# Agent attention and a leaky MLP on one core: the conversions, subtractions and load order of the head, and where the second batch's keys begin

## The chip, the cores and the metric

The kernel runs on 1 core of one Trainium2 chip. The metric is device microseconds of an execution. The kernel before took 1010.07 us as the median of 3 runs (1010.05, 1010.07, 1012.32).

## The reference

```python
scale = 1.0 / np.sqrt(q.shape[-1])
def sm(a, b):
    s = scale * (a @ b.transpose(0, 2, 1))
    s = s - s.max(-1, keepdims=True)
    e = np.exp(s)
    return e / (e.sum(-1, keepdims=True) + 1e-09)
agent_v = sm(agents, k) @ v
x = (sm(q, agents) @ agent_v).reshape(B * S, D)
h = x @ w_in
out = np.maximum(0.01 * h, h) @ w_out
```

q, k and v are (2, 12480, 128) in float32, agents (2, 49, 128). w_in (128 x 2048) and w_out (2048 x 128) arrive as float64 bit patterns and are converted to float32 on the chip.

## The kernel before, in words

The second attention is folded into the MLP. For each batch the kernel needs `agent_v`, multiplies it into `w_in` (m_hi and m_lo, each value split into a rounded part and a rest) and then runs the MLP on 480 queries at a time. There are 26 such blocks per batch, 52 in all, and each is 8 steps of TensorE work. A step is `mm1` (two column tiles of h into a PSUM pair), `relu` (the rounded part on ScalarE, L708, and the rest on VectorE, L709) and, two steps later, `mm2` (L725, L735). A table called `side` hangs all other work on steps. Within a step, mm1 comes first, then the side work, then the mm2 of two steps before.

**The aux tile.** The PSUM pool `ps_x` has one buffer, two banks wide, named aux. The score products of the queries (`q_mm`, L595) take all of it at step 2 of every block. ScalarE then copies one half (`q_x`, L602) and VectorE adds the other (`q_add`, L608), and only then is the buffer free. The second batch's key scores (`k_score`, L359), the transposes of its maximum (`k_max1`, L391; `k_max2`, L403) and the products of its softmax with v (`k_av2`, L451, read by two VectorE additions, L459) use the same buffer.

**The second batch beside the first.** While batch 0's blocks run, one chunk of batch 1's keys is scored per block, at step 5. Then come its maximum and, spread evenly over the steps that remain, 26 halves (13 chunks) of subtraction, exponential and splitting, with `k_av2` 7 steps behind each second half. K1 = 2 of the 13 key chunks are scored already in the head, so 11 blocks carry keys and the 26 halves spread over U = 100 steps, four steps apart.

**The head.** Before the first block everything of batch 0 is made at once. 13 key tiles (480 KB each) are scored on TensorE (L359), VectorE keeps a running maximum (`k_run`, L370), and ScalarE copies the scores (L373). The maximum goes through `k_max0` to `k_max3`. Each chunk then has the maximum subtracted (`k_sub`, L325), its exponential taken (`k_exp`, L417), and is multiplied with its v tile (`k_av32`, L475; 13 tiles of 520 KB). Meanwhile eight tiles of the weights (512 KB each) are converted: `conv_bits` (L242, L243), `conv_exp` (L251, L252), `conv_mant`, `conv_low` (L256), `conv_sign` (L271), `conv_mul` (L278), and `wo_hi_of` for each w_out tile. The first queries go through their own chain (`chain`). At the end `f_copy`, `f_den`, `f_tr`, `f_rec` and `f_avT` finish agent_v, and `m_mm`, `m_hi_of` and `m_lo_of` make m from it. Key, v and weight tiles share nine buffers (`ld`), so a late load waits until an earlier tile has been read.

The order of the head is written by a small planner (`Plan`). Each step has an engine, a cost and the steps it follows; `emit` picks again and again the step that can begin first. The order of loads is given by hand in the string `ORDER`. In the kernel before, a step may have several engines with a cost each, and the planner takes the one that would end first. TensorE's gaps are filled with dummy products (`heat`, L841).

Of the kernel before, what the change touches and what calls it, by code (L numbers as in the profile page):

```python
# [18 lines left out]
class Plan:  # L19
# [6 lines left out]
    def add(self, name, eng, cost, fn, args, after):  # L26
        costs = eng if isinstance(eng, dict) else {eng: cost}
        self.steps[name] = costs, fn, args, after, isinstance(eng, dict)

    def emit(self, engines, idle):  # L30

        tail = {}

        users = {name: [] for name in self.steps}
        for name, step in self.steps.items():
            for a in step[3]:
                users[a].append(name)

        def rest(name):
            if name not in tail:  # L40
                tail[name] = min(self.steps[name][0].values()) + max(
                    (rest(u) + self.hop for u in users[name]), default=0
                )
            return tail[name]

        done = self.done
        while len(done) < len(self.steps):
            best = None
            for name, (costs, fn, args, after, pick) in self.steps.items():
# [3 lines left out]
                end, eng = min((max(ready, self.free[e]) + c, e) for e, c in costs.items())  # L53
                key = max(ready, self.free[eng]), name not in self.first, -rest(name)
                if best is None or key < best[0]:
                    best = key, name, eng, end
            (begin, *_), name, eng, end = best
            _, fn, args, _, pick = self.steps[name]
            if eng == idle[0] and begin > self.free[eng] + idle[2]:
                idle[1](round((begin - self.free[eng]) / idle[2]))  # L60
            fn(*args, *([engines[eng]] if pick else []))
            self.free[eng] = done[name] = end


@with_exitstack
def tile_agent_attention_then_leaky_mlp(
# [55 lines left out]

    ORDER = "kkkwkkkwkkwkkwkkwkwwqvvwvvvvqvvvvvvvq"
    LOWS = "pddddddd"
    K1 = 2
    HOP = 90
# [125 lines left out]
    def conv_low(n):  # L254
# [4 lines left out]
        )  # L259

    def conv_low1(n, eng):
        m_t[n] = rp.tile([P, MC], F32, tag="hi", name="wl")
        scale(eng, m_t[n], w_t[n][:, :, 0].bitcast(U32), 2.0**-52)

    def conv_low2(n):
        w = w_tile(n)
        nc.gpsimd.tensor_tensor(out=w, in0=w, in1=m_t.pop(n), op=ALU.add)

# [516 lines left out]
    for b in range(1, B):  # L785
        i0 = (b - 1) * BPB
        n0 = i0 + NCH - K1
        for c in range(K1, NCH):
            s = NP * (i0 + c - K1)
            for d in range(c, min(c + 3, NCH)) if c == K1 else (c + 2,) if c + 2 < NCH else ():  # L790
# [30 lines left out]
    with tc.manual_schedule():  # L821
# [28 lines left out]
        for o, a, n in SLOTS:  # L850
# [5 lines left out]

        add = plan.add
        fetch = {
            "k": (lambda c: load_k(0, c), 1120), "v": (lambda c: load_v(0, c), 1220),
# [22 lines left out]
        for n in range(2 * NM):  # L882
            r = [("mul", n - RP)] if n >= RP else []
            add(("bits", n), "dve", 900, conv_bits, (n,), [("w", n)] + r)
            add(("mant", n), {"act": 620, "pool": 730}, None, conv_mant, (n,), [("bits", n)])
            add(("exp", n), "act", 1300, conv_exp, (n,), [("bits", n)])
            if LOWS[n] == "d":
                add(("low", n), "dve", 800, conv_low, (n,), [("mant", n)])
            else:
                add(("low1", n), {"act": 620, "pool": 730}, None, conv_low1, (n,), [("mant", n)])  # L890
                add(("low", n), "pool", 1225, conv_low2, (n,), [("low1", n)])
            add(("sign", n), "dve", 900, conv_sign, (n,), [("exp", n)])
            by = {"pool": 1260, "dve": 800}
            add(("mul", n), by, None, lambda n, e: conv_mul(n, e), (n,), [("low", n), ("sign", n)])
            if n % 2:
                add(("wohi", n), {"act": 620, "pool": 730}, None, wo_hi_of, (n,), [("mul", n)])
            if n == 1:
                add(("wolo", n), "dve", 900, wo_lo_of, (n,), [("wohi", n)])
# [15 lines left out]
        add("avopen", "pe", 100, av_zero, (0, True), [])  # L914
        dve, pool, act = nc.vector, nc.gpsimd, nc.scalar
# [25 lines left out]
        for fn, eng, cost, after in (  # L941
            (f_copy, "act", 200, "avend"), (f_den, "pe", 60, f_copy),
            (f_tr, "pe", 220, f_den), (f_rec, "dve", 150, f_den), (f_avT, "act", 160, f_tr),
        ):
            add(fn, eng, cost, fn, (0,), [after] + [("chain", 4)] * (fn is f_den))
        for n in range(NM):
# [15 lines left out]
        plan.emit({"dve": dve, "pool": pool, "act": act}, ("pe", heat, 270))  # L962
        steps = [(i, p) for i in range(NBLK) for p in range(NP)]
# [51 lines left out]
```

## Time and profile before

| | |
|---|---|
| median of 3 runs | 1010.07 us |
| the profiled execution's own time | 1011.78 us |
| its span, first to last instruction | 1010.0 us |
| busy: TensorE products, VectorE, ScalarE, GpSimd | 981.2, 729.8, 599.1, 411.8 us |
| chain that ended last, by engine | PE 89%, DVE 6%, ACT 2% |
| chain that ended last, largest lines | PE o L725 52%, PE h L695 27% |

In the profile PE is TensorE (PEld its weight loads), DVE is VectorE, ACT is ScalarE, POOL is GpSimd and SP the engine whose queue issues the loads. A row of a timeline begins with the start in us, then the duration, and ends in brackets with the idle time of that engine before it and what released it. "L" numbers are lines of the kernel before.

### The profile page before, as it was taken

What the parts mean: (1) busy time and instruction counts of PE and PEld (TensorE: products, weight loads), DVE (VectorE), ACT (ScalarE), POOL (GpSimd) and SP (SyncE); (2) the same over time, 40 slices, a digit from 0 to 9 for tenths busy, and PEclk for the clock granted to TensorE, in tenths of its full rate; (3) what the DMA queues carried; (4) which work ended last, traced back from release to release, by engine and by line L of the source; (5) the groups of instructions that cost most, each with busy time, mean ns of one, the idle gap of its engine ahead of it and who ended that gap; (6) DMA issues with size and microseconds to landing.
All of it is one profiled execution on the core that took longest, in us unless ns stands there. A gap on an engine that the chain in (4) does not pass through costs nothing.

```text
span 1010.0 us, 21532 instructions
## 1 busy us (share of the span) xinstructions
PE 981.2 (97%) x8908; PEld 840.7 (83%) x8908; DVE 729.8 (72%) x1056; ACT 599.1 (59%) x798; POOL 411.8 (41%) x581
## 2 busy tenths in 40 slices
PE   8878999999999999999999999999999999999998
PEld 8756888888878888888887788888888888888886
DVE  6947776776767877778787677777777777777774
ACT  4534555555646666666666566666565656565654
POOL 4732332332326566665655234343333333333320
PEclk9999999999999999999999999999999999999999
DMA  9760121120021121212101001010101010101000
GB/s 354 267 244 1 40 80 40 41 79 21 21 80 40 53 69 41 80 41 64 57 21 40 20 21 41 21 41 20 40 21 41 21 41 20 41 21 41 21 20 21
DMA packets 24029, 57.63 MB, mean 57 GB/s; under 512 B 2787, under 2 KB 16355, under 8 KB 23931
## 3 DMA queue, kind: packets, MB, share of 16 engines
q1 hardware_dynamic: 23787, 56.13, 17.1%
q8 instruction: 70, 1.15, 0.5%
q14 instruction: 28, 0.23, 0.1%
q10 hardware_dynamic: 144, 0.12, 0.0%
HBM read 43.46 MB, written 12.78 MB: 56 GB/s over the span
## 4 chain that ended last, share of the span: by engine, by line
PE 89%; DVE 6%; ACT 2%; issue 1%; DMA 1%; POOL 1%; SPq 0%; POOLq 0%; ACTq 0%; DVEq 0%
PE o L725 52%; PE h L695 27%; PE aux L595 3%; PE aux L359 2%; PE o L735 2%; DVE lo L709 1%; PE aux L451 1%; PE sc L359 1%; DVE s_sb L325 1%; DMA w<-in_w_in_dram 1%; ACT hi L708 1%; PE mp L539 0%; DVE e L243 0%; DVE run L370 0%; PE avw L308 0%
## 5 line engine op out<-in xcount | busy, mean ns | idle before, releaser
L709 DVE SCALAR_TENSOR_TENSOR lo<-h,hi 128x960 fp32r<-128x960 f32 x416 | 481.4, 1157 | 241.6 <-ACT hi L708 235.5
L708 ACT ACTIVATE hi<-h 128x960 fp32r<-128x960 f32 x416 | 405.1, 974 | 324.5 <-PE h L695 321.3
L725 PE MATMUL o<-hi,wo_hi 64*128 64x480 f32 x1664 | 366.3, 384 | 0.8 <-ACT oT L746 0.8
L725 PE MATMUL o<-hi,wo_lo 64*128 64x480 f32 x1664 | 358.0, 376 | 0.0
L695 PE MATMUL h<-pT,m_hi 64*128 64x480 f32 x1664 | 293.5, 378 | 2.3 <-DVE lo L709 1.5
L725 PE MATMUL o<-lo,wo_hi 64*128 64x480 f32 x1664 | 292.2, 376 | 0.0
L725 PEld LDWEIGHTS o<-hi,wo_hi 64*128 64x128 f32 x1664 | 211.1, 184 | 33.9 <-ACT oT L746 9.4
L725 PEld LDWEIGHTS o<-hi,wo_lo 64*128 64x128 f32 x1664 | 211.8, 184 | 22.5
L695 PEld LDWEIGHTS h<-pT,m_hi 64*128 64x128 f32 x1664 | 193.8, 184 | 27.2 <-DVE lo L709 3.1
L725 PEld LDWEIGHTS o<-lo,wo_hi 64*128 64x128 f32 x1664 | 194.9, 184 | 23.5
L695 PE MATMUL h<-pT,m_lo 64*128 64x480 f32 x832 | 201.6, 376 | 0.0
L325 POOL TENSOR_TENSOR qlo<-qt,qhi 128x480 fp32r<-128x480 f32 x52 | 64.5, 1241 | 176.6 <-ACT qhi L579 176.6
L695 PEld LDWEIGHTS h<-pT,m_lo 64*128 64x128 f32 x832 | 114.9, 184 | 11.8
L325 POOL TENSOR_TENSOR pT<-pt,pT 128x480 fp32r<-128x480 f32 x52 | 63.5, 1221 | 138.9 <-ACT pT L676 138.9
L664 POOL TENSOR_TENSOR pd<-d,rs 128x375 f32<-128x375 f32 x52 | 42.9, 826 | 87.2 <-DVE rs L659 81.7
L757 POOL TENSOR_TENSOR oT<-oT 128x480 f32<-128x480 f32 x51 | 62.7, 1229 | 10.6 <-ACT oT L746 10.6
L325 POOL TENSOR_TENSOR d<-st,mm 128x375 f32<-128x375 f32 x52 | 43.4, 834 | 47.3 <-DVE mm L630 47.1
L746 ACT COPY oT<-o 128x960 f32<-128x960 f32 x51 | 49.1, 962 | 20.0 <-PE o L725 20.0
L325 POOL TENSOR_TENSOR vr<-vt,vr 120x512 fp32r<-120x512 f32 x26 | 33.9, 1306 | 13.3 <-DVE vr L320 13.3
L624 POOL COPY sm<-sm 64x15 f32<-64x15 f32 x52 | 10.2, 195 | 71.2 <-DVE sm L644 71.2
L671 DVE STREAM_TRANSPOSE pt<-pd 128x480 f32<-128x480 f32 x52 | 34.8, 670 | 1.4 <-POOL pd L664 1.4
L613 DVE STREAM_TRANSPOSE st<-sq 128x480 f32<-128x480 f32 x52 | 34.7, 667 | 0.0
(134 smaller groups left out, 923.2 us busy)
## 6 DMA issues: line engine op xcount, KB each, us to landing
qt<-in_q_dram SPq DMA_DIRECT2D x53, 240.0 KB, 2.9
kt<-in_k_dram SPq DMA_DIRECT2D x26, 480.0 KB, 6.6
out_dram<-oT SPq DMA_DIRECT2D x51, 240.0 KB, 2.0
vt<-in_v_dram SPq DMA_DIRECT2D x13, 520.0 KB, 5.1
vt<-in_v_dram SPq DMA_DIRECT2D x13, 487.5 KB, 4.7
w<-in_w_in_dram SPq DMA_DIRECT2D x4, 512.0 KB, 7.4
w<-in_w_out_dram SPq DMA_DIRECT2D x4, 512.0 KB, 7.8
out_dram<-oT SPq DMA_DIRECT2D x1, 120.0 KB, 1.7
```

The source lines that it names most:

```text
L325: eng.tensor_tensor(out=o, in0=x, in1=y, op=ALU.subtract)
L359: nc.tensor.matmul(ps[:TP, j * NA:(j + w) * NA], lhsT=k_t[b, c][:, j, :], rhs=a_sb[:, b:b + w, :].rearrange("p b a -> p (b a)"), start=Tru ...
L595: nc.tensor.matmul(ps[:, g, :NB], lhsT=w[b][r], rhs=x[r], start=(n == 0), stop=(n == 2))
L613: nc.vector.transpose(t.rearrange("p n a -> p (n a)"), s_t[i])
L664: nc.gpsimd.tensor_tensor(out=pd[:, :, :A0], in0=d, in1=w.to_broadcast([P, NT, A0]), op=ALU.mult,)
L671: nc.vector.transpose(t, pd.rearrange("p n a -> p (n a)"))
L695: nc.tensor.matmul(ps[:, g, :NB], lhsT=w[b][r, cols(2 * p + g)], rhs=t[r, x], start=(n == 0), stop=(n == 2),)
L708: nc.scalar.activation(hi, ps, AF.Relu)
L709: nc.vector.scalar_tensor_tensor(out=lo, in0=ps, scalar=0.0, in1=hi.bitcast(F32), op0=ALU.max, op1=ALU.subtract,)
L725: nc.tensor.matmul(o[:, g, :NB], lhsT=w[r], rhs=x[r], start=start, stop=stop)
L746: nc.scalar.copy(t, o[:, :, :NB])
L757: nc.gpsimd.tensor_tensor(out=t[:, 0], in0=t[:, 0], in1=t[:, 1], op=ALU.add)
```

## The change

- The planner takes one engine per step. `conv_mant` and `wo_hi_of` run on ScalarE; `conv_low`, `conv_mul` and `k_sub` of the head run on VectorE. The form of `conv_low` on GpSimd (`conv_low1`, `conv_low2`) is gone, and all costs of these steps are other numbers.
- The first block's query chain (`chain`) no longer waits for the maximum of the keys; its first load is the first load of all. The query chain and two weight tiles then stand among the keys.
- K1 is gone: no key chunk of batch 1 is scored in the head, 13 blocks carry keys, and U falls from 100 to 84.
- `ORDER` is another string: four weight tiles among the keys, three after the eighth v tile, the last after the eleventh.

```diff
-    ORDER = "kkkwkkkwkkwkkwkkwkwwqvvwvvvvqvvvvvvvq"
-    LOWS = "pddddddd"
-    K1 = 2
+    ORDER = "qkwkkwkkkkkkwwkkkkvvvvvvvvwwwqvvvwvvq"
...
-        n0 = i0 + NCH - K1
-        for c in range(K1, NCH):
-            s = NP * (i0 + c - K1)
+        n0 = i0 + NCH
+        for c in range(NCH):
+            s = NP * (i0 + c)
...
-        U = (BPB - NCH + K1) * NP - NP - s0 - lag
+        U = (BPB - NCH) * NP - NP - s0 - lag
...
-            add(("bits", n), "dve", 900, conv_bits, (n,), [("w", n)] + r)
-            add(("mant", n), {"act": 620, "pool": 730}, None, conv_mant, (n,), [("bits", n)])
-            add(("exp", n), "act", 1300, conv_exp, (n,), [("bits", n)])
-            if LOWS[n] == "d":
-                add(("low", n), "dve", 800, conv_low, (n,), [("mant", n)])
-            else:
-                add(("low1", n), {"act": 620, "pool": 730}, None, conv_low1, (n,), [("mant", n)])
-                add(("low", n), "pool", 1225, conv_low2, (n,), [("low1", n)])
-            add(("sign", n), "dve", 900, conv_sign, (n,), [("exp", n)])
-            by = {"pool": 1260, "dve": 800}
-            add(("mul", n), by, None, lambda n, e: conv_mul(n, e), (n,), [("low", n), ("sign", n)])
+            add(("bits", n), "dve", 940, conv_bits, (n,), [("w", n)] + r)
+            add(("mant", n), "act", 620, conv_mant, (n, act), [("bits", n)])
+            add(("exp", n), "act", 1440, conv_exp, (n,), [("bits", n)])
+            add(("low", n), "dve", 620, conv_low, (n,), [("mant", n)])
+            add(("sign", n), "dve", 680, conv_sign, (n,), [("exp", n)])
+            add(("mul", n), "dve", 600, conv_mul, (n, dve), [("low", n), ("sign", n)])
...
-                add(("wohi", n), {"act": 620, "pool": 730}, None, wo_hi_of, (n,), [("mul", n)])
+                add(("wohi", n), "act", 620, wo_hi_of, (n, act), [("mul", n)])
...
-                old = [("wcopy", m - 1)] * (m > 0)
-                old += [("mm", 0), f_rec, ("chain", 4)] * (m >= NM - 2)
+                old = [("wcopy", m - 1)] if m else [("chain", 4)]
+                old += [("mm", 0), f_rec] * (m >= NM - 2)
...
-            add(("sub", c), {"dve": 700, "pool": 1090}, None, lambda c, e: k_sub(0, c, e), (c,), after)
+            add(("sub", c), "dve", 490, k_sub, (0, c, dve), after)
...
-            add(("chain", n), eng, cost, fn, (0,), [last] + [k_max3] * (fn is q_mm))
+            add(("chain", n), eng, cost, fn, (0,), [last])
...
-        for c in range(K1):
-            add(("k1", c), "dma", 1120, load_k, (1, c), loads and [loads[-1]] or [])
-            for g in range(4):
-                after = [("k1", c), ("mm", NM - 1)] + ([("t", c - 1, 3), ("t1", c - 1)] if c else [])
-                add(("t", c, g), "pe", 420, k_score, (1, c, g, ps_h, 4), after + ([("t", c, g - 1)] if g else []))
-            add(("t1", c), "dve", 565, k_run, (1, c), [("t", c, 3)])
-            add(("t2", c), "act", 486, k_copy, (1, c), [("t1", c), ("av", 2 * c + 1)])
```

What this does to the order shows at three places. In the changed kernel the line numbers are 14 lower behind the removed functions.

TensorE in the second half of batch 0, before: one block from its step 0 on. aux<-vr,er is `k_av2`, h<-pT is mm1, o<-hi and o<-lo are mm2.

```order
L695 MATMUL h<-pT,m_hi_98 128x480 x4
L695 MATMUL h<-pT,m_lo_99 128x480 x2
L451 MATMUL aux<-vr_110,er_114 113x258 x8
L451 MATMUL aux<-vr_111,er_115 113x258 x8
L725 MATMUL o<-hi,wo_hi 128x480 x2
L725 MATMUL o<-hi,wo_lo 128x480 x2
```

The same place in the changed kernel, block 18 at step 2, where aux<-qhi and aux<-qlo are `q_mm`:

```order
L681 MATMUL h<-pT,m_hi_98 128x480 x4
L681 MATMUL h<-pT,m_lo_99 128x480 x2
L581 MATMUL aux<-qhi,a_hi_94 128x480 x2
L581 MATMUL aux<-qhi,a_lo_96 128x480 x2
L581 MATMUL aux<-qlo,a_hi_94 128x480 x2
L437 MATMUL aux<-vr_110,er_114 113x258 x8
L437 MATMUL aux<-vr_111,er_115 113x258 x8
L711 MATMUL o<-hi,wo_hi 128x480 x2
L711 MATMUL o<-hi,wo_lo 128x480 x2
```

Before, `k_av2` stood at step 0 in each of the 13 blocks 13 to 25. Now the 13 stand at steps 7, 6, 4, 3, 2, 0, 7, 6, 5, 3, 2, 1 and 0 of blocks 14 to 25 (two of them in block 19); at the two steps 2 they come directly behind `q_mm`.

VectorE behind the maximum of the keys (`mb`), before. em and e are `conv_bits`, e<-w `conv_sign`, s_sb `k_sub`.

```order
L408 COPY mb<-aux 120x49
L256 SCALAR_TENSOR_TENSOR w_out_sb<-w_382,w_out_sb 128x512
L325 TENSOR_TENSOR s_sb<-s_sb,mb 120x392 x3
L271 SCALAR_TENSOR_TENSOR e<-w_400,e 128x512
L256 SCALAR_TENSOR_TENSOR w_in_sb<-w_400,w_in_sb 128x512
L242 TENSOR_SCALAR em<-w_446 128x512
L243 TENSOR_SCALAR e<-w_446 128x512
L325 TENSOR_TENSOR s_sb<-s_sb,mb 120x392 x3
```

The same place in the changed kernel:

```order
L394 COPY mb<-aux 120x49
L311 TENSOR_TENSOR s_sb<-s_sb,mb 120x392 x13
L236 TENSOR_SCALAR em<-w_514 128x512
L237 TENSOR_SCALAR e<-w_514 128x512
L236 TENSOR_SCALAR em<-w_548 128x512
L237 TENSOR_SCALAR e<-w_548 128x512
L236 TENSOR_SCALAR em<-w_533 128x512
L237 TENSOR_SCALAR e<-w_533 128x512
L257 SCALAR_TENSOR_TENSOR e<-w_514,e 128x512
L250 SCALAR_TENSOR_TENSOR w_in_sb<-w_514,w_in_sb 128x512
```

All 13 subtractions now stand on VectorE ahead of the last four weight tiles, whose conversions follow; `f_rec` comes behind the `conv_sign` of the last tile. GpSimd had taken 7 of the 13.

The load queue of the changed kernel, up to the last v tile:

```order
L197 DMA qt<-in_q_dram 128x480
L181 DMA kt<-in_k_dram 128x960
L206 DMA w_190<-in_w_in_dram 128x1024
L181 DMA kt<-in_k_dram 128x960 x2
L211 DMA w_229<-in_w_out_dram 128x1024
L181 DMA kt<-in_k_dram 128x960 x6
L206 DMA w_318<-in_w_in_dram 128x1024
L211 DMA w_332<-in_w_out_dram 128x1024
L181 DMA kt<-in_k_dram 128x960 x4
L189 DMA vt<-in_v_dram 128x1040 x8
L206 DMA w_514<-in_w_in_dram 128x1024
```

Behind these stand two more weight tiles, q, three v, the last weight tile and two v. The last eleven v tiles of the kernel before stood behind all eight weight tiles.

## Rows read from the trace of the kernel before

**Rows 1.** What the load queue waited for in the head: us in total, times, longest.

```profile
SPq L195 <- DVE w_out_sb L256: 7.8, 2, 3.9
...
SPq L195 <- DVE w_in_sb L256: 6.8, 2, 6.0
```

**Rows 2.** Windows: us; PE, PEld, DVE, ACT, POOL busy; PEclk, DMA share, GB/s.

```profile
0.00:25.00 25.00, 22.08 (x170) 20.56 (x171) 15.38 (x46) 10.41 (x18) 9.94 (x28) 1.00 0.93 353
20.00:25.00 5.00, 5.00 (x50) 5.00 (x50) 3.87 (x8) 3.27 (x7) 1.66 (x3) 1.00 1.02 415
...
40.50:48.00 7.50, 7.50 (x106) 6.55 (x107) 7.50 (x7) 3.73 (x8) 7.36 (x6) 1.00 0.26 79
```

**Rows 3.** Timeline of TensorE, end of the head.

```profile
58.13 1.09 PE L475 MATMUL avw<-vt,s_sb 120*49 120x130 f32 x16 [1.12 <-DMA vt<-in_v_dram]
...
60.32 0.47 PE L502 MATMUL aux<-sel,avs 113*128 113x128 f32 x2
...
63.42 3.57 PE L539 MATMUL mp<-w_in_sb,avT 128*128 128x512 f32 x4 [2.18 <-ACT avT L514]
...
67.27 1.02 PE L539 MATMUL mp<-w_in_sb,avT 128*128 128x512 f32 x2
...
74.83 0.49 PE L539 MATMUL aux<-ww,avT 128*128 128x128 f32 x2
...
79.34 0.71 PE L695 MATMUL h<-pT,m_hi 64*128 64x480 f32 x4
```

**Rows 4.** Timeline of ScalarE, end of the head.

```profile
63.11 0.26 ACT L514 COPY avT<-aux 128x128 f32<-128x128 f32 x1
67.03 0.69 ACT L560 ACTIVATE m_hi<-mp,rec 128x512 fp32r<-128x512 f32 x1 [3.66 <-PE mp L539]
```

**Rows 5.** Timeline of VectorE in the head.

```profile
34.71 0.57 DVE L370 TENSOR_TENSOR run<-sc,run 120x392 f32<-120x392 f32 x1
35.19 0.68 DVE L256 SCALAR_TENSOR_TENSOR w_in_sb<-w,w_in_sb 128x512 f32<-128x512 uint32 x1
...
39.79 0.21 DVE L408 COPY mb<-aux 120x49 f32<-120x49 f32 x1 [0.20 <-PE aux L403]
...
40.53 3.79 DVE L325 TENSOR_TENSOR s_sb<-s_sb,mb 120x392 f32<-120x392 f32 x3
...
62.66 0.16 DVE L510 RECIPROCAL rec<-den 128x1 f32<-128x1 f32 x1
```

**Rows 6.** Timeline of GpSimd at the same time.

```profile
40.15 7.70 POOL L325 TENSOR_TENSOR s_sb<-s_sb,mb 120x392 f32<-120x392 f32 x6
```

**Rows 7.** Timeline of ScalarE: the output copy L746, at step 2 of successive blocks.

```profile
122.87 0.96 ACT L746 COPY oT<-o 128x960 f32<-128x960 f32 x1 [0.33 <-PE o L725]
141.70 0.96 ACT L746 COPY oT<-o 128x960 f32<-128x960 f32 x1 [0.34 <-PE o L725]
...
604.21 0.96 ACT L746 COPY oT<-o 128x960 f32<-128x960 f32 x1 [0.34 <-PE o L725]
620.99 0.96 ACT L746 COPY oT<-o 128x960 f32<-128x960 f32 x1 [0.34 <-PE o L725]
```

**Rows 8.** One block with `q_mm` and `k_av2`: timelines of TensorE, ScalarE and VectorE.

```profile
420.14 0.48 PE L725 MATMUL o<-hi,wo_hi 64*128 64x480 f32 x2
...
420.84 0.57 ACT L602 COPY sx<-aux 128x480 f32<-128x480 f32 x1
...
422.65 0.62 DVE L608 TENSOR_TENSOR sq<-aux,sx 128x480 f32<-128x480 f32 x1
...
435.39 0.88 DVE L459 TENSOR_TENSOR avs<-aux,avs 113x258 f32<-113x258 f32 x2
```

**Rows 9.** TensorE at the transposed maximum (`k_max2`), step 3 of block 11.

```profile
298.44 0.30 PE L403 MATMUL aux<-dg,ones 49*120 49x49 f32 x1 [0.95 <-DVE sq L608]
```

**Rows 10.** A window of the head's end, and TensorE's longest gap later on.

```profile
64.00:65.00 1.00, 1.00 (x2) 0.34 (x1) 0.00 (x0) 0.00 (x0) 0.48 (x1) 0.50 1.01 402
...
562.31 0.49 PE L539 MATMUL aux<-ww,avT 128*128 128x128 f32 x2 [2.08 <-DVE m_lo L564]
```

More of the change, by code (lines that the diff above doesn't have):

```diff
@@ L26, in add, with emit @@
     def add(self, name, eng, cost, fn, args, after):
-        costs = eng if isinstance(eng, dict) else {eng: cost}
-        self.steps[name] = costs, fn, args, after, isinstance(eng, dict)
-    def emit(self, engines, idle):
+        self.steps[name] = eng, cost, fn, args, after
+    def emit(self, idle):
         tail = {}
@@ L35, in emit @@
         for name, step in self.steps.items():
-            for a in step[3]:
+            for a in step[4]:
                 users[a].append(name)
@@ L40, in rest @@
             if name not in tail:
-                tail[name] = min(self.steps[name][0].values()) + max(
+                tail[name] = self.steps[name][1] + max(
                     (rest(u) + self.hop for u in users[name]), default=0
@@ L48, in emit @@
             best = None
-            for name, (costs, fn, args, after, pick) in self.steps.items():
+            for name, (eng, cost, _, _, after) in self.steps.items():
                 if name in done or any(a not in done for a in after):
@@ L52, in emit @@
                 ready = max((done[a] + self.hop for a in after), default=0)
-                end, eng = min((max(ready, self.free[e]) + c, e) for e, c in costs.items())
                 key = max(ready, self.free[eng]), name not in self.first, -rest(name)
                 if best is None or key < best[0]:
-                    best = key, name, eng, end
-            (begin, *_), name, eng, end = best
-            _, fn, args, _, pick = self.steps[name]
+                    best = key, name
+            (begin, *_), name = best
+            eng, cost, fn, args, _ = self.steps[name]
             if eng == idle[0] and begin > self.free[eng] + idle[2]:
                 idle[1](round((begin - self.free[eng]) / idle[2]))
-            fn(*args, *([engines[eng]] if pick else []))
-            self.free[eng] = done[name] = end
+            fn(*args)
+            self.free[eng] = done[name] = begin + cost
 @with_exitstack
@@ L259, in conv_low @@
         )
[L261 to L267, printed above, removed]
     def conv_sign(n):
@@ L786, in tile_agent_attention_then_leaky_mlp @@
         i0 = (b - 1) * BPB
-        n0 = i0 + NCH - K1
-        for c in range(K1, NCH):
-            s = NP * (i0 + c - K1)
-            for d in range(c, min(c + 3, NCH)) if c == K1 else (c + 2,) if c + 2 < NCH else ():
+        n0 = i0 + NCH
+        for c in range(NCH):
+            s = NP * (i0 + c)
+            for d in range(c, min(c + 3, NCH)) if c == 0 else (c + 2,) if c + 2 < NCH else ():
                 at(s, load_k, b, d)
@@ L857, in tile_agent_attention_then_leaky_mlp @@
         add = plan.add
+        dve, act = nc.vector, nc.scalar
         fetch = {
@@ L883, in tile_agent_attention_then_leaky_mlp @@
             r = [("mul", n - RP)] if n >= RP else []
-            add(("bits", n), "dve", 900, conv_bits, (n,), [("w", n)] + r)
-            add(("mant", n), {"act": 620, "pool": 730}, None, conv_mant, (n,), [("bits", n)])
-            add(("exp", n), "act", 1300, conv_exp, (n,), [("bits", n)])
-            if LOWS[n] == "d":
-                add(("low", n), "dve", 800, conv_low, (n,), [("mant", n)])
-            else:
-                add(("low1", n), {"act": 620, "pool": 730}, None, conv_low1, (n,), [("mant", n)])
-                add(("low", n), "pool", 1225, conv_low2, (n,), [("low1", n)])
-            add(("sign", n), "dve", 900, conv_sign, (n,), [("exp", n)])
-            by = {"pool": 1260, "dve": 800}
-            add(("mul", n), by, None, lambda n, e: conv_mul(n, e), (n,), [("low", n), ("sign", n)])
+            add(("bits", n), "dve", 940, conv_bits, (n,), [("w", n)] + r)
[4 more added lines that the diff above has]
+            add(("mul", n), "dve", 600, conv_mul, (n, dve), [("low", n), ("sign", n)])
             if n % 2:
-                add(("wohi", n), {"act": 620, "pool": 730}, None, wo_hi_of, (n,), [("mul", n)])
+                add(("wohi", n), "act", 620, wo_hi_of, (n, act), [("mul", n)])
             if n == 1:
-                add(("wolo", n), "dve", 900, wo_lo_of, (n,), [("wohi", n)])
+                add(("wolo", n), "dve", 680, wo_lo_of, (n,), [("wohi", n)])
             if n % 2 == 0:
                 m = n // 2
-                old = [("wcopy", m - 1)] * (m > 0)
-                old += [("mm", 0), f_rec, ("chain", 4)] * (m >= NM - 2)
+                old = [("wcopy", m - 1)] if m else [("chain", 4)]
+                old += [("mm", 0), f_rec] * (m >= NM - 2)
                 add(("tr", m), "pe", 880, ww_tr, (m,), [("mul", n)] + old)
@@ L914, in tile_agent_attention_then_leaky_mlp @@
         add("avopen", "pe", 100, av_zero, (0, True), [])
-        dve, pool, act = nc.vector, nc.gpsimd, nc.scalar
         for c in range(NCH):
             after = [k_max3, ("copy", c)]
-            add(("sub", c), {"dve": 700, "pool": 1090}, None, lambda c, e: k_sub(0, c, e), (c,), after)
+            add(("sub", c), "dve", 490, k_sub, (0, c, dve), after)
             add(("e", c), "act", 520, k_exp, (0, c), [("sub", c)])
@@ L944, in tile_agent_attention_then_leaky_mlp @@
         ):
-            add(fn, eng, cost, fn, (0,), [after] + [("chain", 4)] * (fn is f_den))
+            add(fn, eng, cost, fn, (0,), [after])
         for n in range(NM):
@@ L954, in tile_agent_attention_then_leaky_mlp @@
         add("L", "pe", 250, k_m, (0, NM), ["ww", ("mlo", 0)])
-        for c in range(K1):
-            add(("k1", c), "dma", 1120, load_k, (1, c), loads and [loads[-1]] or [])
-            for g in range(4):
-                after = [("k1", c), ("mm", NM - 1)] + ([("t", c - 1, 3), ("t1", c - 1)] if c else [])
-                add(("t", c, g), "pe", 420, k_score, (1, c, g, ps_h, 4), after + ([("t", c, g - 1)] if g else []))
-            add(("t1", c), "dve", 565, k_run, (1, c), [("t", c, 3)])
-            add(("t2", c), "act", 486, k_copy, (1, c), [("t1", c), ("av", 2 * c + 1)])
-        plan.emit({"dve": dve, "pool": pool, "act": act}, ("pe", heat, 270))
+        plan.emit(("pe", heat, 270))
         steps = [(i, p) for i in range(NBLK) for p in range(NP)]
```

## The prediction

> **What bounds the kernel now.** I read the busy shares first: TensorE is busy for 97% of the span, so a microsecond is won only where TensorE waits, and every product put between the blocks costs its full time. The timeline of ScalarE's output copy shows how regular the blocks are: a block that scores one key chunk of the second batch takes 18.83 us (122.87 to 141.70), a block without side products 16.78 us (604.21 to 620.99) [rows 7]. One key chunk therefore costs 2.05 us of block time. What is left to win is the head: the first product of the first block begins only at 79.34 us [rows 3].
>
> What bounds the head is read from its end backwards. The last v tile lands at 58.13, agent_v's transpose ends at 60.79 (60.32 + 0.47), the first product of m begins at 63.42 and m_hi at 67.03, and from there the rest of m, the product of the weights and the two key chunks of the second batch take until 79.34 [rows 3, 4]. Why is the last v tile so late? From 40.5 to 48.0 the loads moved 79 GB/s, where 415 are usual [rows 2]: the load queue had to wait for VectorE to release weight tiles, 7.8 and 6.8 us in four waits [rows 1]. And VectorE was slow there: three subtractions took 3.79 us, 1.26 each, while GpSimd did six of the same form in 7.70 us beside it [rows 5, 6]; an operation of the same width with GpSimd less busy is followed by the next after 0.48 us (34.71 to 35.19) [rows 5]. That operation reads PSUM, so it is not the same one, but 392 elements are 392 elements.
>
> **The change part by part.**
>
> *Loads.* The same tiles are loaded before the last v tile, but eight v tiles now stand ahead of the last four weight tiles, and all tiles that the v loads replace are read early. The tiles up to the last v are 18.0 MB (13 of 480 KB, 13 of 520, 8 of 512, 2 of 240 and the agents). 8.8 MB are moved after 25 us (353 GB/s), and the other 9.2 MB at 415 GB/s take 22.2 us [rows 2]: 47.2, and with a microsecond of latency (an estimate) 48.3 is the early end. The late end is 52.0: only the 6.1 us lost in the gap come back ((1 - 79/415) x 7.5) [rows 2]. I take 49.5, nearer to the count of bytes, because the waits on VectorE were 14.6 us in all [rows 1] and no v load waits for a late weight tile any more. That is 8.6 us earlier than 58.13.
>
> *The query chain.* ScalarE copies avT only at 63.11, though its product ended at 60.79 [rows 3, 4]; ahead of it in ScalarE's order stood the last rounding of the query chain. That chain now runs among the keys. The wait of 2.3 us goes. What could be late next on ScalarE is the rounding of a w_out tile that stands ahead of avT; by the sum for VectorE below its conversion ends near 51, before avT is due.
>
> *TensorE's clock at the end of the head.* The first two products of m took 3.57 us, against 1.02 for a later one, and the granted clock is 0.50 in that stretch, the lower of its two levels [rows 3, 10]. TensorE had waited 2.18 us for avT, after gaps between the v tiles. Without the wait I take the full clock: two products in 1.8 us, so 1.8 us less (bounds 0 and 1.8).
>
> *Key chunks of the second batch, in the head.* Without them the product of the weights' product with avT, at 74.83 [rows 3], begins some 0.4 us sooner and the first block follows it directly: 7.8 us behind m_hi instead of 12.3. That is 4.5 us less.
>
> So the first product of a block would begin at 79.34 - 8.6 - 2.3 - 1.8 - 4.5 = 62.1: 17.2 us of head.
>
> *Does VectorE keep up?* It now does everything that GpSimd did. Behind the maximum (`mb`) stand 13 subtractions at 0.48 (6.2 us) and, up to `f_rec`, most of four weight tiles, at some 2.6 us a tile: 0.6 to 0.68 for each of `conv_low`, `conv_sign` and `conv_mul`, 0.4 for each half of `conv_bits` (estimates from [rows 5]; with little work on GpSimd I take the undisturbed durations). With small waits for ScalarE that is 17.5 us. For m_hi at 54.5, `mb` must come by 36.8. It came at 39.79 [rows 5] with six tiles' conversions ahead of it, slowed by GpSimd; now four tiles and the query chain stand ahead of it, and I estimate 35. The bound is mb at 39.79: `f_rec` at 57.3 and 3 us of the gain lost.
>
> *Key chunks in the blocks.* Two more blocks carry keys: 2 x 2.05 = 4.1 us more [rows 7].
>
> *The spread of the second batch's softmax.* This is a cost the text of the change hides. U = 100 gave 26 halves exactly four steps apart, so `k_av2` stood at step 0 of every block, two steps ahead of the query scores. With U = 84 the distance is 3.36 steps and `k_av2` wanders. The aux tile has one buffer. `q_mm` of step 2 is issued until 420.14; ScalarE's copy follows at 420.84, and VectorE's addition ends at 423.27 (422.65 + 0.62), behind the rest of relu and a transpose [rows 8]. A `k_av2` directly behind `q_mm` waits that long: 3.2 us, twice. At step 3 the wait has a measured neighbour: `k_max2`, at step 3, waited 0.95 us for the same addition [rows 9]; I take 1.1, twice. At step 1 (once) `k_av2` itself holds the buffer: its additions ended at 436.27, about 4 us behind its start, in the block shown [rows 8], and `q_mm` comes 3 us behind: 1.0 us. All other places are free. Together 6.4 + 2.2 + 1.0 = 9.6 us, all on TensorE, with nothing to hide it. The bounds are 4.8 (every wait as the measured 0.95) and, with the clock, the third rival's price.
>
> *Nothing elsewhere.* GpSimd's side work per block grows by a fifth in those blocks, but it is busy for 41% of the span, and each piece has two or more steps of room. The 53 query loads and the maximum of the second batch keep their steps in the block.
>
> **Sum.** -17.2 + 4.1 + 9.6 = -3.5 us. Against the profiled execution's own 1011.78 that is 1008.3; the median of the runs is 1.7 us below that execution, so I predict 1006.6 us.
>
> **The rivals.**
>
> *The waits on aux are short.* If the wandering `k_av2` never waits more than the measured 0.95, the blocks give back 4.8 and the time is 1001.8. For it: this is the only such wait that the trace has. Against it: the addition's place in VectorE's order is the same in every block.
>
> *VectorE alone binds the head: slower.* Its queue is in order, and every weight tile goes to ScalarE and back between `conv_bits` and `conv_sign`. From mb to `f_rec` the kernel before took 22.9 us (39.79 to 62.66) [rows 5]. If it takes as long again and mb stays at 39.8, m_hi begins at 62.9, the first block at 70.7, and the head gains 8.6 where the blocks lose 13.7: 1015.2. This rival decides once `f_rec` is later than 57.7; from 60.7 on the kernel is slower by over 0.3%. For it: VectorE's work in the head grows by some 10 us. Against it: much of the old duration came from GpSimd beside it.
>
> *The clock falls behind the two long waits.* In the trace a wait of 2.18 us stands ahead of a stretch at 0.50, but one of 2.08 us at 562.31, in the midst of dense products, was followed by products of usual length [rows 3, 10]. If each 3.2 us wait costs what the one in the head did, 1.8 us, the time is 1010.2: no change. The Trainium skill, "TensorE: Matmul & The Clock Gate", section "Why this matters for your kernels", warns of idle gaps between bursts of matmuls, since the clock then goes back to half; by that rule this rival is what happens, and the two rows above disagree on it.
>
> **How the numbers follow.** 0.3% is 3.0 us, about what a measurement of this kernel can tell from no change. The forecast has 0.48; its own range, with the loads and VectorE's bounds, is 1003 to 1010.5, and I put 0.26 below 1007.0 and 0.22 above. The short waits have 0.20, the clock 0.12, VectorE 0.20. Faster is 0.26 + 0.20 = 0.46, the same 0.22 + 0.12 = 0.34, slower 0.20. The range reaches from the first rival's time to just short of the second's: 1001.5 to 1014.5.
>
> **What would show it.** Right: no stretch of low DMA share between 40 and 48 us; the last v tile by 50; the first h product at 61 to 64; blocks 11 and 12 at 18.8 us; the blocks with a `k_av2` behind `q_mm` (18 and 23) about 3 us longer than their neighbours, TensorE waiting there for VectorE's sq. Wrong: no wait on sq beyond 1 us at block 18; or `f_rec` later than 55, with ScalarE's m_hi waiting for it; or a granted clock below 1 in blocks 18 and 23.

## The result and the profile after

The changed kernel takes 1021.66 us (median of 4 runs, 1020.44 to 1024.45); four runs of the kernel before give 1011.20. The ratio is 1.0106, with a 95% interval of 1.0076 to 1.0136: slower by about 10 us, where 1006.6 was forecast. The profiled execution took 1020.48 us, its span is 1018.7; the one of before had 1011.78 and 1010.0. The two spans differ by 8.7 us, and that is what the rows have to explain.

The timeline of TensorE at the head's end, which answers to [rows 3]:

```profile
56.89 1.09 PE L461 MATMUL avw<-vt,s_sb 120*49 120x130 f32 x16 [0.19 <-DMA vt<-in_v_dram]
...
60.10 1.99 PE L525 MATMUL mp<-w_in_sb,avT 128*128 128x512 f32 x4
...
62.35 1.02 PE L525 MATMUL mp<-w_in_sb,avT 128*128 128x512 f32 x2
...
69.92 0.70 PE L681 MATMUL h<-pT,m_hi 64*128 64x480 f32 x4
```

The first product of a block begins at 69.92 instead of 79.34: the head did become shorter, by 9.4 us, and not by the 17.2 that were forecast. So the rest of the program is 18.1 us longer (8.7 + 9.4). The last v tile lands at 56.89, only 1.2 us sooner than before.

The windows of the loads, with the columns of [rows 2], and the load queue's waits, as in [rows 1]:

```profile
0.00:25.00 25.00, 21.77 (x153) 19.29 (x153) 17.66 (x53) 12.03 (x21) 6.79 (x27) 1.00 0.91 342
25.00:40.00 15.00, 13.29 (x111) 12.24 (x111) 10.81 (x23) 7.80 (x16) 2.02 (x2) 1.00 0.91 334
40.00:45.00 5.00, 5.00 (x92) 5.00 (x92) 5.00 (x12) 5.00 (x11) 0.00 (x0) 1.00 0.57 163
45.00:56.50 11.50, 7.71 (x106) 7.03 (x102) 7.04 (x16) 8.25 (x15) 1.20 (x1) 0.85 1.00 381
```

```profile
SPq L189 <- PE sc L345: 8.8, 5, 3.4
SPq L181 <- PE sc L345: 8.3, 4, 3.3
SPq L211 <- PE avw L461: 6.2, 2, 5.7
```

The gap of before, 79 GB/s around 45 us, is smaller but not gone: 163 GB/s from 40 to 45. What the queue waits for is new. L211 loads a w_out tile, and avw is the sum of attention times v: for 5.7 us the load waited until the first v tile's products had been done and its buffer was free. They cannot begin before the maximum `mb` is known. The other two lines, 17.1 us in all, are loads that wait until the scores of a key tile are done.

VectorE, which answers to [rows 5]:

```profile
38.52 0.21 DVE L394 COPY mb<-aux 120x49 f32<-120x49 f32 x1 [0.69 <-PE aux L389]
38.76 6.29 DVE L311 TENSOR_TENSOR s_sb<-s_sb,mb 120x392 f32<-120x392 f32 x13
...
47.66 0.43 DVE L236 TENSOR_SCALAR em<-w 128x512 int32<-128x512 int32 x1 [1.93 <-DMA w<-in_w_in_dram]
...
54.21 0.43 DVE L236 TENSOR_SCALAR em<-w 128x512 int32<-128x512 int32 x1 [0.94 <-DMA w<-in_w_out_dram]
...
59.78 0.17 DVE L496 RECIPROCAL rec<-den 128x1 f32<-128x1 f32 x1
```

Thirteen subtractions take 6.29 us, 0.48 each, with GpSimd idle beside them; VectorE then waits for weight tiles that come late. Its last step before m, `f_rec` (the reciprocal), comes at 59.78, but VectorE had waited 0.99 us for TensorE's product just ahead of it, and ScalarE's first m_hi waits for TensorE, not for `f_rec`:

```profile
62.12 0.69 ACT L546 ACTIVATE m_hi<-mp,rec 128x512 fp32r<-128x512 f32 x1 [2.07 <-PE mp L525]
```

The blocks are read from ScalarE's output copy, as in [rows 7], at step 2 of blocks 16 to 19 here:

```profile
376.11 0.96 ACT L732 COPY oT<-o 128x960 f32<-128x960 f32 x1 [0.33 <-PE o L711]
393.88 0.96 ACT L732 COPY oT<-o 128x960 f32<-128x960 f32 x1
412.86 0.96 ACT L732 COPY oT<-o 128x960 f32<-128x960 f32 x1
437.56 0.97 ACT L732 COPY oT<-o 128x960 f32<-128x960 f32 x1 [0.33 <-PE o L711]
```

The intervals are 17.77, 18.98 and 24.70 us, and 17.76 to 17.79 in the kernel before at the same three places. Further on, 509.89 to 533.52 is 23.63. The two key blocks more take 18.8 us each, as forecast. TensorE's timeline, its waits (the whole stretch behind the head) and windows with its granted clock (us, PE busy, PEclk, DMA share, GB/s) show the long one:

```profile
413.53 0.58 PE L581 MATMUL aux<-qlo,a_hi 64*128 64x480 f32 x2
417.25 2.06 PE L437 MATMUL aux<-vr,er 64*113 64x258 f32 x16 [3.14 <-DVE sq L594]
419.12 0.60 PE L711 MATMUL o<-hi,wo_hi 64*128 64x480 f32 x2
...
423.31 0.38 PE L711 MATMUL o<-hi,wo_hi 64*128 64x480 f32 x2
```

```profile
514.27 1.34 PE L437 MATMUL aux<-vr,er 64*113 64x258 f32 x16 [3.13 <-DVE sq L594]
```

```profile
PE aux L437 <- DVE sq L594: 8.2, 4, 3.1
```

```profile
413.00:416.00 3.00, 1.12 (x11) 1.00 0.00 0
416.00:417.00 1.00, 0.00 (x0) 0.61 0.00 0
417.00:418.00 1.00, 0.75 (x6) 0.50 0.00 0
418.00:421.00 3.00, 3.00 (x24) 0.50 0.78 232
421.00:423.00 2.00, 2.00 (x12) 0.50 0.51 148
423.00:425.00 2.00, 2.00 (x20) 0.99 0.00 0
```

`k_av2` (L437) stands directly behind `q_mm` and waits 3.14 us for VectorE's addition (sq); a second one, in block 23, waits 3.13. While TensorE waits, the granted clock falls to 0.50, its lower level (1.2 GHz), and stays there until 423: a product that takes 0.38 us at 423.31 takes 0.60 at 419.12. Against a block with two `k_av2` and no wait (18.74 us, the first experiment below), the interval of 24.70 is 6.0 longer: 3.1 of wait and 2.8 of clock. At 23.63 it is 4.9: 3.1 and 1.8. These prices of the clock are differences; the second experiment tests them.

So the span's 8.7 us are: head -9.4, two key blocks +4.1, waits in the blocks +9.7 (3.14 + 3.13 at step 2; by the intervals, 1.2 twice at step 3 and 1.0 at step 1), half clock behind the two long waits +4.6. The sum is +9.0; another 0.2 is won between the first product and the first output copy, which comes 9.6 us sooner (94.42 instead of 104.04).

### The profile page after: what moved, and what is told of

It reads as the page before. It is cut to its first block, busy times and chain, and to the rows that moved or that the text cites. A ratio compares the mean times of both kernels' runs of the same rounds, so it can differ in the third digit from the quotient of the medians.

```text
span 1018.7 us, 21488 instructions
## 1 busy us (share of the span) xinstructions
PE 984.0 (97%) x8899; PEld 846.2 (83%) x8899; DVE 734.0 (72%) x1071; ACT 604.5 (59%) x806; POOL 384.7 (38%) x557
## 4 chain that ended last, share of the span: by engine, by line
PE 88%; DVE 6%; ACT 3%; DMA 2%; issue 1%; POOL 0%; SPq 0%; POOLq 0%; ACTq 0%; DVEq 0%
PE o L711 50%; PE h L681 26%; PE aux L581 3%; DVE lo L695 3%; PE aux L345 2%; PE o L721 2%; PE sc L345 1%; ACT hi L694 1%; PE aux L437 1%; DMA vt<-in_v_dram 1%; DMA kt<-in_k_dram 1%; PE avw L461 1%; DVE sq L594 0%; DVE pt L657 0%; DVE run L356 0%
```

## The experiments

Each ratio is to runs of the kernel before on the same chip. Their medians, 1012.4 to 1014.2 us, lie some us above those of the first comparison, so ratios are compared, not times alone.

**Where `k_av2` stands.** `e1_av2_moved` changes one line of the changed kernel; steps 1, 2 and 3 become 0, 4 and 4:

```diff
-                at(s + lag, k_av2, b, h // 2)
+                at(s + lag + (0, -1, 2, 1, 0, 0, 0, 0)[(s + lag) % NP], k_av2, b, h // 2)
```

> The changed kernel with one table more: a k_av2 that would stand at step 1 of a block is put at step 0, one at step 2 or 3 at step 4; nothing else is changed. My theory (all that the second batch costs beyond the two key blocks comes from where k_av2 stands: waits of 9.6 us and 4.5 us of half clock behind the two long ones): all 14.1 us go, span 1018.7 - 14.1 = 1004.6, time about 1006.4, faster than the kernel before by 0.5%; no product waits over 1 us for sq, and the granted clock is 1.00 through blocks 18 and 23. Rival (the order of the whole second softmax, its rounding and subtractions on GpSimd and ScalarE, takes the time, not the place of k_av2): most of the 14 us stay, time above 1016. Rival (the two of step 2 alone count): 10.8 us go, time 1009.7.

Measured: 1005.98 us, ratio 0.9943 (0.9921 to 0.9964), span 1003.5. ScalarE's output copies around block 18:

```profile
410.91 0.96 ACT L732 COPY oT<-o 128x960 f32<-128x960 f32 x1
429.65 0.96 ACT L732 COPY oT<-o 128x960 f32<-128x960 f32 x1 [0.33 <-PE o L711]
```

The interval is 18.74 us, the line with L437 is gone from TensorE's waits, and from the first output copy to the last the program is 14.5 us shorter. The place of five of the thirteen `k_av2` accounts for the whole loss in the blocks beyond the two key blocks; the rest of the second softmax, spread as in the changed kernel, costs nothing.

**Wait or clock.** `e2_fill` puts 15 products of zeros between `q_mm` and `k_av2` at the two steps 2:

```diff
+                if (s + lag) % NP == 2:
+                    at(s + lag, fill, (s + lag) // NP)
```

> The changed kernel with 15 more products of zeros (128x480) put between q_mm and k_av2 at the two steps 2 where k_av2 waits for the addition (blocks 18 and 23), written to the output's buffer before that is opened; they do nothing but keep TensorE at work for some 3 us. Theory (a wait of 3.1 us is what takes the clock down, and the half clock costs 2.8 and 1.7 us): the products of k_av2 begin at the same distance behind q_mm, the granted clock stays 1.00 behind them, 4.5 us go: span 1014.2, time about 1016. Rival (the clock falls there for another reason, or the 4.5 us are a wait and not the clock): no gain, time about 1020.5, or up to 3 us longer where the filling is longer than the wait.

Measured: 1017.92 us, ratio 1.0065 (1.0040 to 1.0090). TensorE's timeline, the windows of its clock, and ScalarE's output copies:

```profile
418.12 3.54 PE L732 MATMUL o<-m_lo 128*128 128x480 f32 x15
421.59 1.23 PE L437 MATMUL aux<-vr,er 64*113 64x258 f32 x16
422.64 0.38 PE L711 MATMUL o<-hi,wo_hi 64*128 64x480 f32 x2
```

```profile
418.00:421.00 3.00, 3.00 (x14) 1.00 0.00 0
421.00:424.00 3.00, 3.00 (x34) 1.00 0.43 121
```

```profile
416.94 0.96 ACT L738 COPY oT<-o 128x960 f32<-128x960 f32 x1
439.30 0.96 ACT L738 COPY oT<-o 128x960 f32<-128x960 f32 x1 [0.34 <-PE o L711]
```

The clock stays at 1.00. The interval falls from 24.70 to 22.36, the other from 23.63 to 22.37: 3.6 us together. The filling lasts some 0.3 us longer than each wait (`k_av2` begins 3.98 and 3.99 us behind the start of the last `q_mm` products, in the changed kernel 3.72 and 3.70), so the clock had cost about 4.1; the 4.6 above is what is left by difference. The median fell by 3.7. That the waits take the clock down, and that this costs about what the sum above needs, is shown. The span of its profiled execution, 1019.0, hides it: the head there was 4 us longer, with a wait of 5.91 us for a v tile (3.20 in the changed kernel) and a granted clock of 0.61 between 55 and 60 us. Of the head one execution more or less says little.

**The second batch's keys.** `e3_k1` restores K1 = 2 in the changed kernel, `e4_before_k0` sets it to 0 in the kernel before:

```diff
+    K1 = 2
```

> The changed kernel with the first two key chunks of the second batch scored in the head again, as before (K1 = 2), and with that the even distance of four steps in the second softmax; loads, conversions and subtractions stay as changed. Theory: the head is 4.5 us longer (first product of a block at 74.4), two blocks are 2.05 us shorter each, and the 14.1 us of k_av2 go: span 1018.7 + 4.5 - 4.1 - 14.1 = 1005.0, time about 1006.8, faster than the kernel before by 0.5%. Rival (the head's gain depends on the two chunks being gone, because their buffers or loads then stand in the way of the weights): first product later than 76, time near the kernel before's 1011.

> The kernel before with K1 = 0 alone: no key chunk of the second batch in the head; its loads, its conversions and its subtractions on two engines stay. Theory: the head gains 4.5, two blocks lose 4.1, and k_av2 wanders as in the changed kernel, 14.1: span 1010.0 - 4.5 + 4.1 + 14.1 = 1023.7, time about 1025.5, slower than the changed kernel by 5. If the wandering costs only where the changed head's order stands ahead of it (rival), the time is near 1011.

Measured: `e3_k1` 1008.94 us, 0.9963 (0.9949 to 0.9978); `e4_before_k0` 1025.96, 1.0147 (1.0119 to 1.0174), with the same 8.2 us of waits at `k_av2` and granted clocks of 0.60 and 0.83 behind the first long one. K1 = 0 alone costs 1.4% of the changed kernel (1.0106 against 0.9963) and 1.5% of the kernel before, and turns the changed kernel's gain into a loss. `e3_k1` is 2 us slower than expected: its first product comes at 75.65, in a head whose mean granted clock was 0.66 from 65 to 70 us, and again from 75 to 80.

**Two other parts of the change, each alone in the kernel before.** `e7_before_order` takes the new `ORDER` alone, `e8_before_dve` the engines alone (every choice between GpSimd and another engine becomes the other):

```diff
-    LOWS = "pddddddd"
+    LOWS = "dddddddd"
...
-            add(("sub", c), {"dve": 700, "pool": 1090}, None, lambda c, e: k_sub(0, c, e), (c,), after)
+            add(("sub", c), {"dve": 700}, None, lambda c, e: k_sub(0, c, e), (c,), after)
```

> The kernel before with the changed order of loads alone (K1 = 2, conversions and subtractions on two engines as before). Theory (order and engines have to change together: beside GpSimd a subtraction on VectorE still takes 1.2 us, and the late weight tiles still wait for the first v tile's buffer behind mb): the first product of a block at 78 to 81 against 79.3, time 1010 to 1013. Rival (the order alone carries the head's gain): first product at 75 to 76, time 1007.

> The kernel before with the conversions and subtractions on VectorE and ScalarE alone, its own order of loads and K1 = 2. Theory (the engine beside it makes VectorE slow, so most of the head's gain of 4.9 us that is not the two key chunks' comes from here): 13 subtractions in 6.3 us, the w_out_sb waits of the load queue fall from 14.6 to under 10 us, the first product of a block at 76 to 77, time 1007.5. Rival (VectorE alone is too slow without the new order: mb after 42): first product after 79, time over 1010.

Measured: `e7_before_order` 1009.90 us, 0.9973 (0.9958 to 0.9987), first product at 77.12, between its two cases; `e8_before_dve` 1006.77 us, 0.9938 (0.9919 to 0.9956). VectorE's groups from 38 to 50 us in the latter (count, then busy us, mean ns), and TensorE:

```profile
L325 DVE TENSOR_TENSOR s_sb<-s_sb,mb 120x392 f32<-120x392 f32 x13 | 6.6, 561 | 0.0
```

```profile
57.75 1.99 PE L539 MATMUL mp<-w_in_sb,avT 128*128 128x512 f32 x4
...
74.08 0.71 PE L695 MATMUL h<-pT,m_hi 64*128 64x480 f32 x4
```

The engines alone bring the head's first product from 79.34 to 74.08, more than was expected, and are the largest gain of the three parts that were tried alone. The order adds nothing to it: the changed head with the same keys, `e3_k1`, is no faster. The earlier query chain and the planner's new costs were not tried alone.

**Why the loads came late.** `e5_homes` adds to the first experiment memory of their own for the last four weight tiles, in that of `m_lo` (the dummy products then read their zeros from `wo_lo`):

```diff
+    HOME = 4, 5, 6, 7
...
+        if n in HOME:
+            x = HOME.index(n)
+            t = raw[x // 2][:, x % 2 * 2 * MC:(x % 2 + 1) * 2 * MC]
```

> The first experiment (k_av2 off steps 1 to 3) and with it the last four weight tiles loaded into memory of their own (that of m_lo, which is written only later), so that none of them waits for a v tile's buffer; the order of loads stays. My theory of the head (the gap in the loads was moved, not removed: the second late weight tile waited 5.7 us for the first v tile's buffer, which the maximum mb holds, and all loads behind it waited too): no load waits over 1 us for avw, the share of the loads stays over 0.9 from 40 to 45, the last v tile lands at 52 instead of 56.9, f_rec is then bound by VectorE at about 55 to 56, the first product of a block begins at 66 instead of 69.9; time 1006.0 - 4 = 1002. Rival (the loads are bound by bytes and by the keys' phase, the wait only sits in front of a full queue): last v tile after 56, time 1005 to 1006.5.

Measured: 1004.31 us, 0.9914 (0.9891 to 0.9937). Its windows, with the columns of [rows 2]:

```profile
25.00:40.00 15.00, 13.44 (x112) 12.37 (x114) 10.81 (x23) 7.80 (x16) 2.04 (x2) 1.00 0.92 326
40.00:45.00 5.00, 5.00 (x94) 5.00 (x94) 5.00 (x12) 4.99 (x12) 0.00 (x0) 1.00 1.02 411
45.00:55.00 10.00, 7.70 (x114) 7.24 (x111) 9.06 (x18) 8.48 (x14) 1.96 (x1) 0.85 1.03 407
```

The gap is gone, so its cause was the buffer. But v's last products end at 55.8 instead of 57.3 in the first experiment, and the first product comes at 67.73 against 69.28: 1.6 us, less than half of what was expected. Behind 40 us the loads now run at the full 410 GB/s; what was lost earlier, at 326 GB/s from 25 to 40, cannot be made up.

**The order with the memory.** Three more kernels change only `ORDER` in `e5_homes`. `e6_homes_w` has six weight tiles ahead of the v tiles, the last two far back; in `e9_homes_w2` these stand behind six v tiles; `e10_homes_w3` has five and three:

```diff
-    ORDER = "qkwkkwkkkkkkwwkkkkvvvvvvvvwwwqvvvwvvq"
+    ORDER = "qkwkkwkkkwkkwkkwkkkwvvvvvvvvvqvvwvvwq"
...
+    ORDER = "qkwkkwkkkwkkwkkwkkkwvvvvvvwwqvvvvvvvq"
...
+    ORDER = "qkwkkwkkkkwkkkwkkkwvvvvvvwwwqvvvvvvvq"
```

> The kernel with four weight tiles in memory of their own and another order of loads: two more weight tiles ahead of the v tiles, so that VectorE converts six tiles, not four, before mb (it idles some 11 of the first 40 us). Theory (behind the loads VectorE's work after mb is the next bound: 13 subtractions of 0.48 and two tiles of 2.6 instead of four): mb at most 1 us later, f_rec at about 52 to 53, the first product at 63, time 999. Rival (mb itself is pushed behind the two conversions by as much as is saved after it, or the last v tile binds): first product at 66, time 1002.

> The last experiment but with the last two weight tiles put behind six v tiles instead of eleven and twelve: nothing then stands in the load queue behind a v tile that waits for a buffer, except v tiles. Theory (that experiment failed because the load queue is in order: its tenth v tile waited 6.7 us for the first v tile's buffer, and the last two weight tiles behind it landed at 51 and 55): no wait of over 3 us for avw, the share of the loads from 40 to 45 over 0.8 instead of 0.28, the last weight tile landed before 48, the last v tile's products begun by 52, the first product of a block at 64, time about 1000.5. Rival (mb at 39.6 and the bytes bind): the last v tile's products begin after 54, first product at 67, time 1003.5 or more.

> As the other kernel of this call, with five instead of six weight tiles ahead of the v tiles and three behind the sixth, so that VectorE converts one tile less before mb. Theory: mb at 38.4 to 39 (39.6 with six), VectorE has three tiles (7.8 us) and the subtractions (6.3 us) behind it, about even: first product at 64 to 65, time 1000.5 to 1001.5. Rival (what counts is VectorE's work behind mb): first product a tile later, 2.6 us behind that of the other kernel.

Measured: `e6_homes_w` 1012.48 us, 0.9995 (0.9985 to 1.0005), a clear miss: the tenth v tile waited 6.7 us for a buffer, the two weight tiles stood behind it in the queue, and VectorE idled 3.64 us for the first of them. `e9_homes_w2` 1004.06 us, 0.9920 (0.9892 to 0.9948); `e10_homes_w3` 1007.61, 0.9941 (0.9922 to 0.9959), another miss: its products with v ended at 52.5, but TensorE then waited 2.85 us for ScalarE's copy of avs, the granted clock was 0.50 from 57 to 60, and its first product came at 69.77. What made that copy late was not looked into. In `e9_homes_w2` the loads came as early as was expected, though a v tile still waited 6.3 us for a buffer, and the head gained nothing by it (windows, the load queue's longest wait and TensorE's timeline):

```profile
25.00:40.00 15.00, 14.00 (x108) 12.34 (x107) 12.89 (x28) 8.96 (x18) 2.79 (x4) 1.00 1.03 412
...
50.00:55.00 5.00, 4.00 (x62) 3.63 (x57) 3.34 (x4) 2.69 (x6) 2.95 (x2) 1.00 0.05 17
```

```profile
SPq L190 <- PE avw L469: 7.7, 4, 6.3
```

```profile
41.26 11.73 PE L469 MATMUL avw<-vt,s_sb 120*49 120x130 f32 x208
52.93 0.33 PE L462 MATMUL avw<-wo_lo 120*128 120x130 f32 x1
...
55.74 3.12 PE L535 MATMUL mp<-w_in_sb,avT 128*128 128x512 f32 x4 [0.31 <-ACT avT L508]
...
68.35 0.71 PE L691 MATMUL h<-pT,m_hi 64*128 64x480 f32 x4
```

The loads are done at 50, with 412 GB/s also during the keys. Now the 208 products of attention and v bind: 11.73 us without a gap, from 41.26 on, because they cannot begin before `mb`. Behind them the chain to the first product takes 15.4 us (52.93 to 68.35) where `e5_homes` needed 12.0 from 55.74, at a clock that falls twice, between 56 and 60 and between 63 and 67. This execution took 1007.71 us, the other three 1003.79 to 1004.06, so its clock says little of those; against `e5_homes` it lost 2.9 us at the change of the batch (last section).

**The clock at the head's end.** `e11_heat2` adds products of zeros in the two gaps ahead of m, `e12_heat4` also around the fourth transpose of the weights:

```diff
+        for n, dep, user in ((4, "avend", f_den), (3, f_tr, ("mm", 0))):
+            add(("heat", dep), "pe", 220 * n, heat, (n,), [dep])
+            plan.steps[user][4].append(("heat", dep))
```

> The kernel with six weight tiles ahead of the v tiles and two behind the sixth, and with five products of zeros more: three behind the last v tile's products, two behind the transpose of agent_v, where TensorE waited 1.0 and 0.3 us for ScalarE. Theory (at the head's end the half clock comes behind such gaps: there it was 0.50 to 0.72 from 56 to 60 and 0.50 to 0.66 from 63 to 67, some 4 us in all): the first two products of m take 2 us instead of 3.1, the first stretch at 0.50 is gone, the first product of a block 1.5 to 2 us sooner, at 66.5; time 1002.3. Rival (the gaps are too small to matter, the clock falls for the work being thin as a whole): no change, first product at 68, or 0.5 later by the filling.

> As the other kernel of this call, with four and three products of zeros also around the fourth transpose of the weights (61 to 63), where TensorE waited 0.9 and 0.7 us; the planner then puts half of the weights' product ahead of the fourth product of m. Theory: the second stretch at 0.50 (63 to 67) goes too, another 1.5 to 2 us: first product at 64.5 to 65, time 1000.5. Rival (the changed order makes the weights' product wait for its copy and costs what the clock gives): first product at 67 to 68, time 1003.

Measured: 1004.11 us, 0.9906 (0.9879 to 0.9932), and 1004.27, 0.9906 (0.9880 to 0.9932). In `e11_heat2` the first slow stretch is gone (granted clock 1.00 from 55 to 63), and the first two products of m take 1.98 us instead of 3.12; the second stretch, at 0.50 from 64 to 67, stays. But this execution began its products with v 1.1 us later than that of `e9_homes_w2`, and its first block's product came at 68.38, as without the filling. On the clock the reading is plain, on the time it is inconclusive: neither kernel came near the 1002.3 and 1000.5 that were expected. Of `e12_heat4` there is no trace of an execution near its median, so whether its second pair of fillings held the clock is open.

The best versions, `e5_homes`, `e9_homes_w2`, `e11_heat2` and `e12_heat4`, lie together at 1004.1 to 1004.3 us, by their ratios 0.8 to 0.9% under the kernel before, where the changed one is 1.1% above it.

## Why the prediction was wrong

Two terms failed, both of them in the same direction; every other term of the sum came out.

*The loads, "That is 8.6 us earlier than 58.13": 1.2 measured.* The step said that no v load waits for a late weight tile any more, and that all tiles that the v loads replace are read early. It did not ask which buffers the late tiles take over. With nine buffers in turn, three of the last four weight tiles and the last five v tiles take over v tiles' buffers, and these stay full until `mb`. `e5_homes` shows it for the weight tiles: with other memory the gap is gone. The step also took 415 GB/s for everything behind 25 us, a rate from a stretch in which nothing waited. Against that rate the changed kernel lost 0.7 us of loading before 25 ((415 - 342) x 25 / 415 = 4.4, of which 3.7 were in the forecast's own 353), 2.9 between 25 and 40, 3.0 in the gap and 0.9 behind it: 7.5, about the 7.4 between the landing at 56.9 and the forecast's 49.5. In the stretch of those 2.9 us the v loads wait until a key tile's scores are done, 7.6 us in four waits; `e9_homes_w2`, with weights between the keys, had 412 GB/s in that stretch. And the whole term could not have been cashed in: `e9_homes_w2` had its loads done by 50, and then the products with v ended no sooner than 52.9. This cover, TensorE's 11.7 us behind `mb`, was not in the prediction; with `mb` at the forecast's 35 it would have fitted (35.2, 2.1 to the first product as in `e9_homes_w2`, and 11.7 are 49.0, an estimate). The microsecond of latency in the early end of the loads came from no row, and no run here measures it; the landing at 56.9 lies behind both ends of the forecast, 48.3 and 52.0.

*The clock.* The rival that the clock falls behind the two long waits was left out of the sum, with a chance of 0.12 and a price of 3.6; it happened, and cost 4.6 by difference, 4.1 by the filling. It was weighed by two rows, a wait of 2.18 us with the clock at 0.50 behind it and one of 2.08 without [rows 3, 10]. Both are a microsecond shorter than the waits that it was to judge, so the second row was no evidence against it. The Trainium skill, "TensorE: Matmul & The Clock Gate", section "Why this matters for your kernels", which warns of idle gaps between bursts of matmuls, was right here: 0.50 behind 3.14 us of wait, 1.00 where the gap is filled.

With these two put right the sum is -3.5 + 7.4 + 4.6 = 8.5, against 8.7 measured.

What held: the wait for avT (2.1 us gained between the last v tile's landing and the first product of m, 2.3 forecast); the clock at m (1.99 us for two products instead of 3.57, 1.6 gained of 1.8); the key chunks in the head (from m_hi to the first block's product 7.80 us instead of 12.31, exactly 4.5); two more key blocks (4.1); and the waits of `k_av2` place by place, 9.7 us in sum where 9.6 was forecast, 3.14 and 3.13 at step 2 where 3.2 stood. The subtractions took 0.48 us each, as a row of another operation had suggested. `mb` came at 38.52, not at 35: the last of TensorE's key scores begins only at 34.7, and the bound of 39.8 was the better guess. What held the keys up was not taken apart. The rival that VectorE alone binds the head, at 1015.2, stood nearest to the measured time; its head was nearly right too (first block at 70.7, 69.92 measured; `f_rec` behind 57.7, 59.78 measured). That was luck: VectorE waited for tiles and for TensorE, m_hi waited for TensorE's product, and `e8_before_dve` shows that VectorE alone is the part of the change that gains.

## What to carry to other kernels

When a load is moved, ask of every tile that is loaded behind it whose buffer it takes, and when that buffer's last reader can run; a gap in the loads otherwise moves instead of going. When a distance that happened to divide the period evenly is changed (100 steps in 25 pieces, 84 in 25), follow each piece to the place in the period where it lands, and price the wait there: here one constant decided over 14 us. And price a wait on TensorE together with the slower products behind it.

## What the runs showed of the hardware

VectorE and GpSimd on the same form slow each other: a subtraction on VectorE took 1.26 us beside GpSimd's, which took 1.28 each [rows 5, 6], and 0.48 alone. Moving all of it to the one engine gained 0.6% in `e8_before_dve`. The Trainium skill, "SBUF — State Buffer", section "Who interferes with whom", says that a VectorE instruction with two SBUF inputs contends with a GpSimd instruction that reads SBUF, for a pair of ports that is locked exclusively. The direction agrees with 1.26 and 1.28 us per operation side by side. Strict turns would need more: a GpSimd subtraction of the same form takes 0.96 in a block (at 429.52 in the kernel before), and 0.48 + 0.96 is 1.44.

The clock does not fall behind every equal wait. At the change of the batch, in the last product of m, `e5_homes` and `e9_homes_w2` wait equally long (timeline and windows of each in turn, us, PE busy, PEclk, DMA share, GB/s):

```profile
554.50 0.49 PE L535 MATMUL aux<-ww,avT 128*128 128x128 f32 x2 [2.08 <-DVE m_lo L560]
```

```profile
556.00:560.00 4.00, 4.00 (x40) 1.00 0.00 0
```

```profile
555.12 0.80 PE L535 MATMUL aux<-ww,avT 128*128 128x128 f32 x2 [2.09 <-DVE m_lo L560]
```

```profile
556.00:560.00 4.00, 4.00 (x20) 0.50 0.01 2
```

The first block goes on at the full clock, the second at half of it, and takes 28.13 us instead of 25.19. What decides between the two, these runs do not show. Executions of one and the same program lie up to 4 us apart here (1020.44 to 1024.45 for the changed kernel); that such falls of the clock make the difference is likely, but was not shown.
